# A gated mix of two attentions on one core: shift transfers one at a time, and the last four output rows spread over the last steps

## The chip, the cores and the metric

The kernel runs on one core of one Trainium2 chip. The metric is the device time of one execution in microseconds (us). Before the change it is 1537.48 us as the median of three runs (1534.87 to 1542.45). The engines of the core are TensorE (PE; its weight loads are PEld), VectorE (DVE), ScalarE (ACT), GpSimd (POOL) and SyncE (SP), which here only issues transfers.

## The reference

Both branches read the same `x` of 2048 rows by 512. Branch A is a sliding, dilated attention: each row attends to eight rows, itself and every second one behind it. Branch B is full attention of 32 query heads over one shared key and value head. A gate per row mixes the two outputs.

```python
S, D, H, Dh = 2048, 512, 32, 16
g = sigmoid((x * gate_w).sum(-1, keepdims=True))
# A: q, k, v per head from x @ wqkv; W = 8, dilation 2
logits = einsum("bhsd,bhswd->bhsw", q, k[pos - 2*w]) * Dh**-0.5   # masked where pos - 2*w < 0
a = (softmax(logits) weighted sum of v[pos - 2*w]) @ wo
# B: q per head from x @ wq, one k and v from x @ wk, x @ wv
b = (softmax(q @ k.T * Dh**-0.5) @ v) @ wo_b
return g * a + (1 - g) * b
```

Everything is float32. The queries and keys of B are large, so its softmax needs the row maximum taken off before the exponential.

## The kernel before

Float32 products of full accuracy are made from rounded parts: a high and a low half of each operand, and three products (high with high, high with low, low with high) added up in PSUM.

**Projections (to about 291 us).** A list of lumps, `lumps`, runs through the function `stream`: fourteen query lumps, then the lumps `("a", gg, j)`, where `gg` counts four groups of columns of branch A and `j` sixteen groups of 128 rows. A lump is twelve steps. In each step the two halves of the 128 contraction rows go as two matmuls on the two halves of the array (line 956) into the two halves of a PSUM pair, so the two halves must be added later. `a_post` does that after each lump: for the group `gg == 0` (which also carries the values of B and the gate's sums) ACT copies one half (line 241) and DVE adds the other half to it, three additions (lines 246, 248, 249). For the later groups `a_add` has ACT copy both halves (lines 265, 266) and POOL add them (line 272). The sum goes into a `stage` tile, of which there are two, each for two lumps, and every second lump the tile is stored to the DRAM buffer `ad`: from ACT's queue for group 0 (line 253), from SP's queue for the others (line 276). Branch A itself is computed later on POOL from `ad`.

**Maxima of branch B.** The scores of B are computed twice: once to find the maximum of each query row, once for the exponential. The first time is cut into 2048 *fills*; a fill is one 128 by 512 block of scores (line 330) and a reduction on DVE. They are not tied to a place: `stream` and the main loop put them wherever their planner finds a free PSUM bank. `fill_pair` does two at once in the bank `m2` (reduction line 350), `fill_one` a single one in the bank `m1` or another (line 361). During the projections of A another form is used, a *difference pass*: `fill_diff` forms half differences of two key blocks, ACT takes absolute values (line 418), and `fill_sum` adds half sums and reduces (line 428), so that one pass covers four fills. A unit `v` (there are 32, a quarter of the queries by four heads) has 64 fills. When they are done, `filled` sends its maxima through `shift_a` and `shift_c` (ACT, then POOL, which forms the tile `ml`) to `shift_b`, which writes them into rows 62 and 63 of the stacked queries `qst` by eight small transfers (line 449), issued at once. While branch A occupies POOL all eight go on SP's queue, later four on each. The exponentials of the unit may only start when its shift has been issued (`shifted`).

**Branch B.** The main loop has 512 steps and one more, sixteen for each unit. In a step `exp_pair` runs twice (scores on PE, line 460, exponential on ACT, line 462), and `weighted` adds the step before to the output (line 470, bank `po`). `fill_ready` adds up to one pair and one single fill a step. If the next unit's maxima would come too late, `pause` makes fills without exponentials. After each unit `finish_a`, `finish_b` and `finish_c` divide, gate and transpose its output; a unit is then `shaped`.

**Output rows.** `out_phase` multiplies four groups of 128 rows at a time with the output weights, as a block in which no exponential runs. For a row group, `prepare` splits branch B's part, `turn` transposes branch A's part, the products run through `stream` as two half matmuls each (line 731), with fills in between, and `out_store` has ACT copy both halves (line 666) and POOL add them. There are four blocks. In the last, the column block of the last two units is not yet there: its four sums are kept in `parts`, and the end of the kernel adds what is missing (line 1073) and stores.

**What sets the order.** The instruction order of each engine is written out by the planner when the program is built. It keeps planned clocks (`clk`, and `pool` for POOL), free times of banks (`free`) and a list `tasks` of due times, which `run_tasks` works off; it does not see the real times. Each engine and each queue then runs strictly in the written order.

## Time and profile before

| what | value |
|---|---|
| median of three runs | 1537.48 us |
| the profiled execution, its own time | 1539.43 us |
| span of its trace | 1537.6 us |
| mean granted clock of TensorE | 0.992 |
| PE, DVE, ACT, POOL busy | 1491.8, 1250.2, 1232.9, 1016.9 us |
| chain that ended last: PE, DVE, ACT, POOL | 85%, 5%, 4%, 2% |

The trace gives each instruction a start and a duration. Busy time is the time in which an engine executes; registers, semaphores and the issue of transfers are not counted. A matmul's record is longer than the distance to the next one, because matmuls overlap in the array: 0.40 us is listed for one that starts 0.24 us after its predecessor, so starts are to be compared. A wait names the instruction, what it waited for, the sum, the count and the longest, in us. Where the engine `SPq` or `POOLq` stands, it is the issue of a transfer. "Granted clock" is the share of its full rate at which TensorE was let run.

### The profile page before, as it was taken

What the parts mean: (1) busy time and instruction counts of PE and PEld (TensorE: products, weight loads), DVE (VectorE), ACT (ScalarE), POOL (GpSimd) and SP (SyncE); (2) the same over time, 40 slices, a digit from 0 to 9 for tenths busy, and PEclk for the clock granted to TensorE, in tenths of its full rate; (3) what the DMA queues carried; (4) which work ended last, traced back from release to release, by engine and by line L of the source; (5) the groups of instructions that cost most, each with busy time, mean ns of one, the idle gap of its engine ahead of it and who ended that gap; (6) DMA issues with size and microseconds to landing.
All of it is one profiled execution on the core that took longest, in us unless ns stands there. A gap on an engine that the chain in (4) does not pass through costs nothing.

```text
span 1537.6 us, 29033 instructions
## 1 busy us (share of the span) xinstructions
PE 1491.8 (97%) x11020; PEld 717.7 (47%) x11020; DVE 1250.2 (81%) x1794; ACT 1232.9 (80%) x1532; POOL 1016.9 (66%) x1725
## 2 busy tenths in 40 slices
PE   7999988999999999999999999999999999999997
PEld 4989878633333333333333453333453354333532
DVE  6987555688888889888898998888998899888821
ACT  4547766888999999999999759999759966998676
POOL 7833867888978888888988988888886132000320
PEclk9999989999999999999999999999999999999999
DMA  6743223220120211211211112202110000000000
GB/s 214 203 116 130 74 73 94 79 75 22 65 70 16 85 51 43 68 46 40 75 40 41 67 39 68 62 18 68 41 57 22 2 15 16 2 2 1 2 1 28
DMA packets 43908, 85.63 MB, mean 56 GB/s; under 512 B 9520, under 2 KB 25960, under 8 KB 39672
## 3 DMA queue, kind: packets, MB, share of 16 engines
q1 hardware_dynamic: 31976, 40.85, 8.9%
q0 software_dynamic: 6560, 37.95, 7.3%
q10 hardware_dynamic: 5232, 4.98, 1.0%
q8 instruction: 86, 1.41, 0.4%
q14 instruction: 54, 0.44, 0.1%
HBM read 57.97 MB, written 25.25 MB: 54 GB/s over the span
## 4 chain that ended last, share of the span: by engine, by line
PE 85%; DVE 5%; ACT 4%; POOL 2%; SPq 1%; DMA 1%; issue 1%; DVEq 0%; ACTq 0%; POOLq 0%
PE po L470 32%; PE pe L460 22%; PE pm L330 9%; PE ps L330 8%; PE pe L956 5%; PE pe L731 5%; ACT pexp L462 3%; DVE mx L350 3%; DVE mx L361 2%; SPq L449 1%; PE pe L174 1%; PE pm L409 1%; POOL stage L272 1%; DMA ad<-stage 1%; ACT dd L418 1%
## 5 line engine op out<-in xcount | busy, mean ns | idle before, releaser
L462 ACT ACTIVATE pexp<-pe 128x1024 f32<-128x1024 f32 x1024 | 991.7, 1022 | 98.8 <-PE pe L460 95.9
L350 DVE TENSOR_REDUCE mx<-pm 128x2 f32<-128x1024 f32 x563 | 687.1, 1220 | 125.1 <-PE pm L330 120.2
L470 PE MATMUL po<-pexp,vst 128*32 128x512 f32 x4096 | 545.5, 605 | 1.0 <-DVE tt L484 0.5
L460 PE MATMUL pe<-qst,kst 64*128 64x512 f32 x2048 | 464.8, 450 | 9.8 <-ACT pexp L462 4.8
L460 PEld LDWEIGHTS pe<-qst,kst 64*128 64x128 f32 x2048 | 191.3, 183 | 514.1 <-ACT pexp L462 500.5
L361 DVE TENSOR_REDUCE mx<-ps 128x1 f32<-128x512 f32 x568 | 385.8, 679 | 5.5 <-PE ps L330 4.7
L330 PE MATMUL pm<-kst,qst 62*128 62x512 f32 x1139 | 239.7, 408 | 2.3 <-DVE mx L350 1.8
L330 PE MATMUL ps<-kst,qst 62*128 62x512 f32 x568 | 230.6, 406 | 0.8 <-DVE mx L361 0.8
L530 POOL TENSOR_TENSOR pr<-aext 128x256 f32<-128x256 f32 x256 | 182.6, 741 | 2.6 <-DMA aext<-ad 2.4
L590 POOL TENSOR_TENSOR oa<-oa,av 128x256 f32<-128x256 f32 x224 | 164.3, 733 | 15.1
L470 PEld LDWEIGHTS po<-pexp,vst 128*32 128x32 f32 x4096 | 80.5, 108 | 179.4 <-issue 166.4
L587 POOL TENSOR_TENSOR av<-aext,lg 128x256 f32<-128x256 f32 x224 | 139.6, 623 | 13.5
L496 POOL TENSOR_TENSOR rl<-rl,gate_t 128x16 f32<-128x16 f32 x31 | 6.9, 222 | 180.5 <-DVE rl L490 180.3
L330 PEld LDWEIGHTS pm<-kst,qst 62*128 62x128 f32 x1139 | 110.4, 186 | 27.2 <-DVE mx L350 23.1
L330 PEld LDWEIGHTS ps<-kst,qst 62*128 62x128 f32 x568 | 105.7, 186 | 25.6 <-DVE mx L361 20.6
L956 PE MATMUL pe<-wah,xh 64*128 64x384 f32 (+1 forms) x504 | 112.0, 349 | 3.0 <-DVE gate L249 1.7
L956 PE MATMUL pe<-wah,xl 64*128 64x384 f32 (+1 forms) x504 | 112.7, 347 | 0.0
L428 DVE CUSTOM_DVE_ANT_0 dd<-ps,dd 128x512 f32<-128x512 f32 x78 | 53.9, 691 | 71.6 <-PE ps L409 36.9
L956 PE MATMUL pe<-wal,xh 64*128 64x384 f32 (+1 forms) x504 | 111.9, 345 | 0.0
L418 ACT ACTIVATE dd<-pm 128x512 f32<-128x512 f32 x156 | 85.3, 600 | 28.6 <-PE pm L409 26.5
L536 POOL TENSOR_TENSOR tr<-pr 128x512 f32<-128x512 f32 x64 | 81.7, 1277 | 4.3
L536 POOL TENSOR_TENSOR tr<-tr 128x256 f32<-128x256 f32 (+1 forms) x128 | 72.5, 567 | 8.6
(172 smaller groups left out, 1582.4 us busy)
## 6 DMA issues: line engine op xcount, KB each, us to landing
aext<-ad POOLq DMA_DIRECT2D x32, 1056.0 KB, 5.5
ad<-stage SPq DMA_DIRECT2D x24, 384.0 KB
qst<-qd SPq DMA_DIRECT2D x64, 128.0 KB
xraw<-xt SPq DMA_DIRECT2D x16, 256.0 KB
qd<-qhi SPq DMA_DIRECT2D x16, 256.0 KB
qd<-qlo SPq DMA_DIRECT2D x16, 256.0 KB
qst<-qd SPq DMA_DIRECT2D x64, 64.0 KB
qst<-ml SPq DMA_DIRECT2D x228, 2.0 KB
```

The source lines that it names most:

```text
L330: nc.tensor.matmul(dst, qst[v % NB][b:b + 62, pr, t * P:(t + 1) * P], kst[b:b + 62, kc * 512:(kc + 1) * 512], start=True, stop=True)
L350: nc.vector.tensor_reduce(m[:, :, pr, t, kc], dst, AX.X, ALU.max)
L361: nc.vector.tensor_reduce(m[:, odd, pr, t, kc:kc + 1], dst, AX.X, ALU.max)
L418: nc.scalar.activation(dd[0][:, odd], m2[:, odd, :], AF.Abs)
L460: nc.tensor.matmul(bank[:, odd, :], kst[b:b + 64, kt * P:(kt + 1) * P], qst[u % NB][b:b + 64, pr, :], start=True, stop=True)
L462: nc.scalar.activation(e, bank, AF.Exp, scale=SCALE)
L470: nc.tensor.matmul(po[32 * i:32 * i + 32, :], vst[:, kt, :], pexp[s, i // 2][:, i % 2, :], start=(kt == 0), stop=(kt == NJ - 1))
L530: nc.gpsimd.tensor_mul(pr[:, k], q, e[:, o:o + NH, AC:2 * AC])
L536: nc.gpsimd.tensor_add(nx, cur[:, :, 0:n], cur[:, :, n:2 * n])
L587: nc.gpsimd.tensor_mul(av, e[:, o:o + NH, 2 * AC:].rearrange("p j (h d) -> p j h d", d=DH), lg[:, w].unsqueeze(3).to_broadcast([P, NH, AG, ...
L590: nc.gpsimd.tensor_add(ao, ao, av)
L956: nc.tensor.matmul(front[2 if x == last else x % 2][0][:, b, :n], l[h], r[h], start=(i == 0), stop=(i == 3 * C - 1))
```

## The change

There are four edits.

1. `a_post` treats group 0 as it treats the others: ACT copies both halves to SBUF (and the narrow columns of the values and of the gate by two more copies), POOL adds them (three additions), and the store goes out on SP's queue. The planned durations become 1.2 us on ACT and 1.45 us on POOL. The old path through DVE, its tasks `post0` and `post1`, and the store on ACT's queue go away.
2. `shift_b` no longer issues its eight transfers at once. During the projections each becomes a task of its own, due 0.8 us after the one before (`shift_d`); in the main loop they are still issued together. The unit counts as shifted with the eighth.
3. In `stream`, a difference pass may be started when DVE's planned clock is up to 1.2 us ahead of PE's, in place of 0.7.
4. The last four row groups are no longer an `out_phase`. A generator, `spread`, gives out their products four at a time in each step of the main loop, as full 128-row matmuls into the two halves of `m2`, once all fills are done; `turn_all` transposes with four full transposes through `m1`, and ACT copies the finished row straight into `parts`. What is left after the last step runs then. The rule for single fills, now `singles`, is set to finish the fills at about step 488 of 512.

```diff
     def a_post(gg, j, x):
-        for kind in ("post0", "post1", "add") if not gg else ("post0", "post1"):
-            settle(kind, 0)
+        settle("add", 1)
...
         nc.scalar.activation(own, bank[:, 0, :GN].rearrange("p (g n) -> p g n", g=GC), AF.Copy)
-        nc.scalar.activation(two, bank[:, 1, :GN], AF.Copy)
-        at = after("act", clk["pe"] + T_LAT, 0.8)
+        nc.scalar.activation(two[:, :n], bank[:, 1, :n], AF.Copy)
+        if gg == 0:
+            nc.scalar.activation(vst[:, j, 0:DH], bank[:, 0, GN:GN + DH], AF.Copy)
+            nc.scalar.activation(gate[:, 1, j:j + 1], bank[:, 0, GN + DH:GN + DH + 1], AF.Copy)
+        at = after("act", clk["pe"] + T_LAT, 0.8 if gg else 1.2)
...
     def shift_b(v, ml):
-        for b in range(2):
-            dst = qst[v % NB][64 * b + 62:64 * b + 64].rearrange("x i (t q) -> x i t q", t=4).bitcast(F32)
-            for g in range(4):
-                (nc.gpsimd if b and not pieces else nc.sync).dma_start(...)
-        shifted.add(v)
+        for k in range(8):
+            if pe:
+                shift_d(v, ml, k)
+            else:
+                tasks.append((clk["pe"] + 0.8 * k, shift_d, (v, ml, k)))
...
-                if not half and not pend and max(free["m2"], clk["dve"] - 0.7) <= clk["pe"] + 0.1:
+                if not half and not pend and max(free["m2"], clk["dve"] - 1.2) <= clk["pe"] + 0.1:
                     fill_diff()
...
+    def spread(js, n):
+        m = 3 * (C + n)
+        def turn_all(j):
+            for c in range(C):
+                nc.tensor.transpose(m1[:, c * P:(c + 1) * P], oa[c // 2][:, j, c % 2 * P:(c % 2 + 1) * P], ident)
...
+        prepare(js[0], n)
+        yield 1.0
+        parts_a(js[0], *turn_all(js[0]))
+        yield 3.0
+        while slots or half:
+            yield 1.0
+        for j in js:
...
+                nc.tensor.matmul(m2[:, j % 2, :], st(), mv, start=(i == 0), stop=(i == m - 1))
...
+                if i == m - 6 and nxt:
+                    raw = turn_all(nxt)
+                yield 0.0
...
+            nc.scalar.activation(parts[j], m2[:, j % 2, :], AF.Copy)
...
+    def singles(s):
+        return 2 * max(0, 16 * (NU - 1) - 8 - s) + 11 * (NJ - 4 - outs) < to_go()
...
+        if outs == NJ - 4:
+            if NU - 3 in shaped and not half and not singles(s) and not later_rows and "last" not in done:
+                later_rows.append(spread(list(range(outs, NJ)), n))
+            if short > 0 and steps < 2:
+                pause(short)
...
-                ahead = 2 * (16 * (NU - 2) - 8 - s) + 11 * (NJ - 4 - outs)
-                if ahead < to_go() - NF // NU or s >= 16 * (NU - 2) - 8 and ahead + 64 < to_go():
+                if not later_rows and singles(s):
                     fill_ready("m1", M1S)
...
+        spread_some(4)
         if s:
             weighted(s - 1)
...
+    while later_rows:
+        clk["pe"] = max(clk["pe"], spread_at[0])
+        spread_some(99)
+        run_pool()
```

More of the change, by code (lines that the diff above doesn't have):

```diff
@@ L271, in rest @@
             nonlocal pool
-            nc.gpsimd.tensor_add(own, own, two.rearrange("p (g n) -> p g n", g=GC))
-            pool = max(pool, 1e3 * at) + 1000
+            nc.gpsimd.tensor_add(own, own, two[:, :GN].rearrange("p (g n) -> p g n", g=GC))
+            if gg == 0:
+                nc.gpsimd.tensor_add(vst[:, j, 0:DH], vst[:, j, 0:DH], two[:, GN:GN + DH])
+                nc.gpsimd.tensor_add(gate[:, 1, j:j + 1], gate[:, 1, j:j + 1], two[:, GN + DH:GN + DH + 1])
+            pool = max(pool, 1e3 * at) + (1000 if gg else 1450)
             if j % 2 == 1:
@@ L660, in gated_mix_kernel, with out_store @@
     parts, spare = {}, []
-    def out_store(j, n, k):
+    def out_store(j, k):
         nonlocal pool
@@ L668, in out_store @@
         pool = max(pool, 1e3 * clk["act"]) + 1300
[L669 to L680 removed]
+        nc.gpsimd.tensor_add(two[:, 0], two[:, 0], two[:, 1])
+        nc.sync.dma_start(out[0].rearrange("(p j) d -> p j d", j=NJ)[:, j, :], two[:, 0])
     def stream(seq, mm, done, pooled):
@@ L994, in gated_mix_kernel @@
     formed.clear()
-    for kind in ("post0", "post1", "add", "store"):
+    for kind in ("add", "store"):
         settle(kind, 0)
@@ L1047, in gated_mix_kernel @@
         run_pool()
-    assert not slots and not half and not hooks and not tasks and outs == NJ, (len(slots), len(hooks), len(tasks), outs)
+    while later_rows:
+        clk["pe"] = max(clk["pe"], spread_at[0])
+        spread_some(99)
+        run_pool()
+    assert not slots and not half and not hooks and not tasks and "last" in done, (len(slots), len(hooks), len(tasks), outs)
     for x in range(8):
```

93 lines of the change are left out of this document (53 added, 40 removed).

## The prediction

> **What bounds the kernel now.** I began with the page: share of busy time by engine, then the chain that ended last.
>
> ```profile
> PE 1491.8 (97%) x11020; PEld 717.7 (47%) x11020; DVE 1250.2 (81%) x1794; ACT 1232.9 (80%) x1532; POOL 1016.9 (66%) x1725
> ```
>
> TensorE (PE) is busy for 97% of the span, so a gain comes either from stretches where PE stands still, or from PE work that can lie under another engine. The change touches two places, so I went on with those: the projections of branch A (84 to 291 us) and everything behind the last sixteen-row unit (1412 us to the end).
>
> First place. The waits between 150 and 291 us have one entry that belongs to no engine:
>
> ```profile
> ACT stage L265 <- DMA ad<-stage: 18.5, 4, 7.0
> ```
>
> The same view of 158 to 172 us and of 282 to 300 us has the shortest two:
>
> ```profile
> ACT stage L265 <- DMA ad<-stage: 3.2, 1, 3.2
> ```
> ```profile
> ACT stage L265 <- DMA ad<-stage: 2.0, 1, 2.0
> ```
>
> Four times ScalarE (ACT) waits, 18.5 us in all, for a stage tile whose store to `ad` has not landed: 3.2, 7.0, 6.3 (what is left of the sum) and 2.0 us. The queue of SyncE (SP) says why (start, duration, what was issued; neighbours are merged):
>
> ```profile
> 158.16 5.23 SPq L449 DMA_DIRECT2D qst<-ml  x8
> 163.49 21.54 SPq L276 DMA_DIRECT2D ad<-stage  x5
> 195.70 5.22 SPq L449 DMA_DIRECT2D qst<-ml  x8
> 200.97 29.07 SPq L276 DMA_DIRECT2D ad<-stage  x6
> ...
> 276.18 5.56 SPq L449 DMA_DIRECT2D qst<-ml  x8
> 281.79 14.05 SPq L276 DMA_DIRECT2D ad<-stage  x4
> ```
>
> Four batches of eight small shift transfers (the one left out starts at 238.04) hold SP for 5.2 us each, 0.65 us per transfer, and a store is issued the moment the batch ends. ACT's own row answers it: issue at 200.97, work again at 203.77, so 2.8 us from issue to a free tile.
>
> ```profile
> 203.77 0.49 ACT L265 ACTIVATE stage<-pe 128x384 f32<-128x384 f32 x1 [7.01 <-DMA ad<-stage]
> ```
>
> What that does to PE is in busy time by stretch (busy us of PE, PEld, DVE, ACT, POOL, then the granted clock): the four batches, then a stretch without one.
>
> ```profile
> 157.00:177.00 20.00, 17.03 (x152) 16.04 (x150) 8.98 (x29) 13.46 (x31) 14.99 (x27) 0.83 0.24 71
> 195.00:215.00 20.00, 13.59 (x116) 12.91 (x116) 7.69 (x24) 9.17 (x21) 10.45 (x26) 0.74 0.27 81
> 237.00:257.00 20.00, 14.24 (x131) 13.60 (x129) 8.09 (x26) 10.21 (x22) 11.37 (x18) 0.83 0.36 115
> 276.00:291.00 15.00, 12.90 (x130) 11.75 (x128) 8.09 (x27) 11.16 (x24) 10.84 (x16) 1.00 0.26 81
> 215.00:235.00 20.00, 20.00 (x216) 19.40 (x214) 13.10 (x42) 17.92 (x41) 17.34 (x24) 1.00 0.23 70
> ```
>
> PE idles 3.0, 6.4, 5.8 and 2.1 us there, 17.3 us together, and not at all without a batch. After the three longer stops its clock is low as well:
>
> ```profile
> 168.70 0.52 PE L956 MATMUL pe<-wah,xl 64*128 64x384 f32 x2
> 169.02 0.52 PE L956 MATMUL pe<-wah,xh 64*128 64x384 f32 x2
> ...
> 174.50 0.34 PE L956 MATMUL pe<-wah,xl 64*128 64x384 f32 x2
> 174.67 0.34 PE L956 MATMUL pe<-wah,xh 64*128 64x384 f32 x2
> ```
>
> The pace is 0.32 us a pair at 168.70 and 0.17 at 174.50. Some 5.9 us from 168.1 on run at about half pace, a loss of 2.7 us; for three stops 8 us. After the fourth, whose wait was 2.0 us, the clock stayed at 1.00.
>
> Second place, the ordinary step of branch B while score maxima (fills) are still being placed, on PE:
>
> ```profile
> 1377.37 0.50 PE L460 MATMUL pe<-qst,kst 64*128 64x512 f32 x2
> 1377.70 0.40 PE L330 MATMUL pm<-kst,qst 62*128 62x512 f32 x2
> 1377.94 0.40 PE L460 MATMUL pe<-qst,kst 64*128 64x512 f32 x2
> 1378.18 0.40 PE L330 MATMUL ps<-kst,qst 62*128 62x512 f32 x1
> 1378.51 1.06 PE L470 MATMUL po<-pexp,vst 128*32 128x512 f32 x8
> 1379.50 0.50 PE L460 MATMUL pe<-qst,kst 64*128 64x512 f32 x2
> ```
>
> Start to start: 0.33 for scores, 0.24 for a pair of maxima, 0.24 for scores, 0.33 for a single one, 0.99 for the weighted sum, 2.13 us with no gap: PE-bound, three maxima a step. In the last steps the maxima are gone and ACT is the bound, two steps every 4.02 us:
>
> ```profile
> 1473.33 3.77 ACT L462 ACTIVATE pexp<-pe 128x1024 f32<-128x1024 f32 x4 [0.18 <-PE pe L460]
> 1477.35 3.77 ACT L462 ACTIVATE pexp<-pe 128x1024 f32<-128x1024 f32 x4 [0.25 <-PE pe L460]
> ```
>
> So 2.01 us a step, in which PE needs 0.33 + 0.24 + 0.99 = 1.56. Between the two regimes stands the block that the change dissolves: weighted sum 483, then number 484, with these reductions of maxima inside it.
>
> ```profile
> 1441.01 1.06 PE L470 MATMUL po<-pexp,vst 128*32 128x512 f32 x8
> ...
> 1471.79 1.07 PE L470 MATMUL po<-pexp,vst 128*32 128x512 f32 x8
> ```
> ```profile
> L350 DVE TENSOR_REDUCE mx<-pm 128x2 f32<-128x1024 f32 x13 | 15.9, 1226 | 0.4 <-PE pm L330 0.3
> L361 DVE TENSOR_REDUCE mx<-ps 128x1 f32<-128x512 f32 x14 | 9.5, 682 | 0.6 <-PE ps L330 0.6
> ```
>
> The block lasts 30.8 us, of which 2.0 would have been an ordinary step: 28.8 us. It also carries 2 x 13 + 14 = 40 maxima. Those have to go somewhere else.
>
> **The change part by part.** *Shift transfers one at a time.* In the projections the eight transfers become tasks 0.8 us apart, so a store that falls due gets its place after the first or second, not after the eighth. The count on SP stays 8. The first still waits on POOL for `ml`, and a store behind it waits too. Each store is then issued six to seven transfers earlier, 3.9 to 4.6 us. Of the four waits 3.2 and 2.0 vanish, the others shrink by about 4.6: 14.4 us. What remains (2.4 and 1.7) is near the 2.0 after which the clock stayed up, so I count all 8 us of low clock as saved. Term: -22.4. Bounds: all idle and all low clock gone, -25.3; a store that comes only one transfer earlier, -2.6.
>
> *Sums of the first A group from VectorE (DVE) to ACT and POOL; their stores from ACT's queue to SP's.*
>
> ```profile
> L241 ACT ACTIVATE two<-pe 128x402 f32<-128x402 f32 x16 | 8.1, 509 | 12.5 <-PE pe L956 6.3 <-DMA ad<-stage 3.6 <-DVE gate L249 2.1
> L246 DVE TENSOR_TENSOR stage<-pe,two 128x384 f32<-128x384 f32 x16 | 8.8, 549 | 0.8 <-ACT two L241 0.8
> L272 POOL TENSOR_TENSOR stage<-stage,two 128x384 f32<-128x384 f32 x48 | 48.7, 1016 | 22.1 <-ACT two L266 21.9
> ```
> ```profile
> 105.00:132.00 27.00, 26.68 (x269) 25.46 (x267) 21.64 (x78) 19.03 (x39) 3.78 (x6) 1.00 0.23 73
> ```
>
> DVE loses 0.55 us and two narrow adds per position, ACT gains a copy of 0.49 (the row at 203.77) and two narrow ones (0.9 us together, an estimate: no row has copies so narrow from PSUM), POOL gains an add of 1.02 and two narrow ones. POOL is busy 3.8 of 27 us there, so its work is hidden, and DVE was not the bound. ACT is at 19.0 of 27; about ten positions at 0.9 us bring it to 28, just over the stretch. I charge 2 us (0 if copies overlap, 9 if all of the 0.9 went on the path). The eight stores leave ACT's queue; on SP they meet only spread shifts.
>
> *The margin in the planner for difference passes (0.7 to 1.2), and the DVE time freed,* change how many maxima are placed before branch B. By the planner's own durations: 0.75 us freed in each of the first six positions at about 0.6 per maximum, +8; a pass that starts a step earlier, 5 passes of four in 48 positions, +20; ACT planned 1.2 instead of 0.45 in the first group, -10 to -15. I take +15 (0 to +35). Each pass costs PE about 0.3 us: +1.5 in all.
>
> *Four rows spread over the last steps.* The block goes: -28.8. The 84 products (21 for each row) become full 128-row matmuls, four a step. The nearest row, for the same shape:
>
> ```profile
> 1526.40 2.11 PE L1052 MATMUL pm<-woh 128*128 128x512 f32 x8
> ```
>
> Eight end to end take 2.11, the last one's length included: about 0.24 each. A step is then 0.33 + 0.24 + 4 x 0.24 + 0.99 plus two changes of tile shape at 0.09 (0.33 less 0.24 above), 2.70 us, PE-bound. For ACT, the copies of a row:
>
> ```profile
> L639 ACT ACTIVATE raw<-pe 128x512 f32<-128x512 f32 x16 | 9.6, 598 | 42.4 <-PE pe L633 39.2 <-POOL own L626 3.3
> ```
>
> Four of about this size in 21 / 4 steps are 0.46 a step, and the exponentials 3.77 / 2 = 1.89: 2.35, just beneath PE. So 21 steps x (2.70 - 2.01) = +14.5. [...] Were a change free, the term would be 21 x 0.51 = +10.7, and if ACT and PE did not overlap in half of the steps' copies, +19. Transposes and first preparation: +2. What is left after step 512: +1.4.
>
> *The 40 maxima of the block.* The new rule for singles (`2 x (488 - step) < to go`) lets twelve steps, 477 to 488, take one: +0.12 each, 1.5 us, and steps 485 to 488 take eight in pairs at no cost. Twenty are left at step 489, three fit, 17 go into a pause. A pause has been seen, five maxima long:
>
> ```profile
> 1412.86 1.06 PE L470 MATMUL po<-pexp,vst 128*32 128x512 f32 x8
> ...
> 1418.06 0.64 PE L470 MATMUL po<-pexp,vst 128*32 128x512 f32 x4
> ```
>
> 5.20 less 2.13 is 3.07 us, 0.61 per maximum. So 17 cost +10.4. The 15 gained above take off 9.2 (first the old pause of five, then ten of these).
>
> Sum: -22.4 + 2 + 1.5 - 28.8 + 14.5 + 2 + 1.4 + 1.5 + 10.4 - 9.2 = -27.1 us. The profiled execution took 1539.4 (span 1537.6 and 1.8 around it), so 1512.3; the median shown, 1537.48, is 1.9 lower, which would give 1510. I predict 1512.
>
> **The rivals.** *The tail gives nothing back.* No maxima are gained in front, 17 wait at step 489, and in that pause of some 10 us PE does a pair per 1.2 us. Then -9.2 and -1.5 fall away, and ACT's copies cost another 2: 1522. If so sparse a stretch drops the clock once, add the 2.7 of one stop above: 1524. [...] Chance 0.16.
>
> *The stores do not come earlier,* because the planner gives a store its place behind all eight, which its due time (up to 2.5 us ahead on POOL, plus 0.5) would allow if shifts go out in a bunch. For it: SP runs in written order. Against: tasks 0.8 us apart reach over 5.6 planned us, more than two lumps. Term -2.6 instead of -22.4: 1532. Chance 0.11.
>
> *Slower: the maxima run short.* Place: a pause at step 489 and the one at 473. Price 0.61 each. If ACT's longer duty in the first group lets the planner place fewer difference passes there (four maxima each), the pause grows. It decides from 27 / 0.61 = 44 missing, eleven passes: 1540 and above, say 1547 at 14. Against it: the margin of 1.2 works the other way in the 48 later positions. Chance 0.07.
>
> *Better:* all stops and both pauses gone: 1500 and less. Chance 0.04.
>
> **How the numbers follow.** The forecast has 0.62, reaching from 1500 to 1526 by the ends of its terms. Range 1500 to 1532: outside lie 0.04 below, 0.07 above for the shortage, and about half of the 0.11. A measurement of this kernel tells a change from none at about 0.5%, 7.7 us: faster means under 1530, slower over 1545. Faster: 0.62 + 0.16 + 0.03 of the second rival = 0.81, with 0.04 for better 0.85; I keep 0.82, since more than one term is unseen in any trace. Same: 0.11. Slower: 0.07.
>
> **What would show it.** Right: on SP no eight `ml` transfers in a row between 150 and 291 us; ACT's wait on `ad<-stage` under 5 us; granted clock 1.00 there; no block near the end, and 2.6 to 2.8 us a step in some 20 of the last 24 steps; reductions of maxima ended by about step 490. Wrong: the wait of 18.5 still there; PE gaps of over 10 us at step 489; steps of 3 us or more with products; the branch B loop starting later than before.

## The result, and the profile after

The changed kernel takes 1526.99 us as the median of six runs (1525.66 to 1528.23); the kernel before, in six runs beside it, 1537.49. The ratio is 0.9928, with a 95% interval of 0.9912 to 0.9945: faster by 10.5 us, which is more than the 0.5% that a measurement can tell, inside the range given, just beyond the 1526 us to which the forecast itself reached, and less than half of the 25.5 us forecast.

The profiled execution of the changed kernel took 1525.66 us, its span is 1523.8. One mark cuts the span in two: the transpose of the first unit's output (`tt<-po`). Up to it run the projections and the first unit; behind it run the other 31 units and the end of the kernel. Before, then after, from the timeline of DVE:

```profile
329.57 0.70 DVE L484 STREAM_TRANSPOSE tt<-po 128x512 f32<-128x512 f32 x1
```
```profile
314.37 0.71 DVE L472 STREAM_TRANSPOSE tt<-po 128x512 f32<-128x512 f32 x1
```

So the front gave 15.2 us, and the rest went from 1537.6 - 329.6 = 1208.0 to 1523.8 - 314.4 = 1209.4: the dissolved block brought nothing. My sum had -18.9 for the front (-22.4 + 2 + 1.5) and -8.2 for the rest. The two spans differ by 13.8 us and the medians by 10.5, because the profiled execution of the kernel before is 1.9 us above its median and that of the changed kernel 1.3 below.

**The front.** The waits between 150 and 291 us, one row of the kernel before, then two of the changed kernel:

```profile
PEld pm L409 <- ACT dd L418: 17.1, 6, 6.7
```
```profile
PEld pm L390 <- ACT dd L399: 11.6, 32, 1.6
...
ACT stage L240 <- DMA ad<-stage: 1.7, 2, 1.6
```

The 18.5 us of ACT's wait for the stage tile are 1.7. The row above it has changed its nature: PE's weight load for a difference pass waited 6 times for ACT to read the bank of the pass before, up to 6.7 us at a time, and now waits 32 times, 0.36 us each. The queue of SP shows a store inside a shift where eight transfers stood together:

```profile
191.76 3.91 SPq L436 DMA_DIRECT2D qst<-ml  x6
195.78 0.36 SPq L257 DMA_DIRECT2D ad<-stage  x1
196.19 1.26 SPq L436 DMA_DIRECT2D qst<-ml  x2
```

And the busy time by stretch (PE, PEld, DVE, ACT, POOL, then the granted clock) has no low clock any more, but PE now also idles 1.0 us from 215 to 235 us, where it was busy throughout before:

```profile
157.00:177.00 20.00, 19.78 (x200) 17.67 (x198) 13.22 (x42) 18.27 (x43) 17.96 (x33) 1.00 0.24 72
...
215.00:235.00 20.00, 18.97 (x192) 16.96 (x188) 12.77 (x42) 15.78 (x36) 16.24 (x26) 1.00 0.41 128
```

**The tail.** A step with products, on PE:

```profile
1453.63 1.06 PE L458 MATMUL po<-pexp,vst 128*32 128x512 f32 x8
1454.63 0.73 PE L448 MATMUL pe<-qst,kst 64*128 64x512 f32 x4
1455.29 0.73 PE L766 MATMUL pm<-wol,own 128*128 128x512 f32 x2
1455.86 0.63 PE L766 MATMUL pm<-woh,own 128*128 128x512 f32 x2
1456.42 1.06 PE L458 MATMUL po<-pexp,vst 128*32 128x512 f32 x8
```

2.79 us from start to start, without a gap: 1.00 for the weighted sum, 0.66 for four score products, 1.13 for four output products. The forecast was 2.70. Three times, where a row ends, the step is longer, by 2.2, 2.0 and 1.7 us. PE and ACT at the first of these places:

```profile
1466.81 1.94 ACT L450 ACTIVATE pexp<-pe 128x1024 f32<-128x1024 f32 x2 [0.84 <-PE pe L448]
...
1466.87 0.49 PE L766 MATMUL pm<-woh,turned 128*128 128x512 f32 x1
1468.63 0.60 ACT L781 ACTIVATE part<-pm 128x512 f32<-128x512 f32 x1
...
1469.29 0.97 PE L766 MATMUL pm<-woh,own 128*128 128x512 f32 x3 [1.92 <-ACT part L781]
```

The row's last product starts at 1466.87. The copy of the finished row (line 781) stands on ACT behind two exponentials and begins at 1468.63. The next row's first product goes into the other half of the bank pair `m2`, which nothing else uses then, but it starts only when the copy has ended. The waits of the end (1400 to 1525 us) have the sum:

```profile
PEld pm L766 <- ACT part L781: 6.2, 3, 2.2
PE pm L766 <- ACT part L781: 5.1, 3, 1.9
```

The second loss lies at the pause of fills ahead of the last unit, at step 488. PE, then the clock of the stretches around it:

```profile
1437.85 0.80 PE L448 MATMUL pe<-qst,kst 64*128 64x512 f32 x2 [1.77 <-DVE mx L331]
```
```profile
1434.00:1438.00 4.00, 1.91 (x13) 0.82 (x9) 3.72 (x5) 1.73 (x2) 0.00 (x0) 0.91 0.00 0
1438.00:1442.00 4.00, 4.00 (x16) 1.37 (x16) 0.69 (x1) 1.26 (x2) 0.00 (x0) 0.50 0.01 4
1442.00:1446.00 4.00, 4.00 (x25) 0.74 (x22) 1.19 (x3) 2.86 (x4) 0.00 (x0) 0.73 0.00 0
```

After a stop of 1.77 us PE ran at half rate for some 6.4 us (1437.85 to about 1444.2), a loss of 3.2 us.

### The profile page after: what moved, and what is told of

It reads as the page before. It is cut to its first block, busy times and chain, and to the rows that moved or that the text cites. A ratio compares the mean times of both kernels' runs of the same rounds, so it can differ in the third digit from the quotient of the medians.

```text
span 1523.8 us, 28901 instructions
## 1 busy us (share of the span) xinstructions
PE 1489.5 (98%) x10920; PEld 706.1 (46%) x10920; DVE 1235.3 (81%) x1755; ACT 1243.8 (82%) x1590; POOL 1030.6 (68%) x1769
## 4 chain that ended last, share of the span: by engine, by line
PE 89%; ACT 4%; DVE 4%; POOL 1%; issue 1%; DMA 1%; DVEq 0%; ACTq 0%; POOLq 0%
PE po L458 32%; PE pe L448 22%; PE pm L311 9%; PE ps L311 8%; PE pe L1004 8%; PE pe L709 4%; DVE mx L331 2%; ACT dd L399 2%; ACT pexp L450 1%; PE pm L766 1%; PE pm L390 1%; PE pe L174 1%; DVE mx L342 1%; PE po L390 0%; PE ps L390 0%
## 5 line engine op out<-in xcount | busy, mean ns | idle before, releaser
L331 DVE TENSOR_REDUCE mx<-pm 128x2 f32<-128x1024 f32 x554 | 676.6, 1221 | 125.7 <-PE pm L311 120.4
L311 PE MATMUL pm<-kst,qst 62*128 62x512 f32 x1122 | 235.7, 407 | 3.1 <-DVE mx L331 2.4
L311 PEld LDWEIGHTS ps<-kst,qst 62*128 62x128 f32 x565 | 105.3, 186 | 22.4 <-DVE mx L342 18.4
L399 ACT ACTIVATE dd<-pm 128x512 f32<-128x512 f32 x166 | 92.2, 610 | 21.8 <-DVE mx L409 10.8
L1004 PE MATMUL pe<-wah,xh 64*128 64x384 f32 (+1 forms) x504 | 108.5, 338 | 0.0
L1004 PE MATMUL pe<-wal,xh 64*128 64x384 f32 (+1 forms) x504 | 108.5, 337 | 0.0
L1004 PE MATMUL pe<-wah,xl 64*128 64x384 f32 (+1 forms) x504 | 108.4, 337 | 0.0
L409 DVE CUSTOM_DVE_ANT_0 dd<-ps,dd 128x512 f32<-128x512 f32 x83 | 57.4, 692 | 58.8 <-PE ps L390 29.4
L250 POOL TENSOR_TENSOR stage<-stage,two 128x384 f32<-128x384 f32 x64 | 65.0, 1015 | 26.3 <-ACT two L241 13.4
```

The costliest lines, as they stand in the source:

```text
L311: nc.tensor.matmul(dst, qst[v % NB][b:b + 62, pr, t * P:(t + 1) * P], kst[b:b + 62, kc * 512:(kc + 1) * 512], start=True, stop=True)
L331: nc.vector.tensor_reduce(m[:, :, pr, t, kc], dst, AX.X, ALU.max)
L399: nc.scalar.activation(dd[0][:, odd], m2[:, odd, :], AF.Abs)
L1004: nc.tensor.matmul(front[2 if x == last else x % 2][0][:, b, :n], l[h], r[h], start=(i == 0), stop=(i == 3 * C - 1))
```

## The experiments

Twelve more kernels were run. "First unit" is the mark above, "rest" the span less that mark; both come from the one profiled execution, and two executions of the same front differ by up to 2 us (314.4, 314.6 and 316.5 in the table; the last one, of e5, has the granted clock at 0.71 and 0.87 from 92 to 100 us, where the other two have 1.00). "Passes" is the number of difference passes in the program; each does the work of four fills. Ratios are to the kernel before, with their 95% intervals.

| kernel | passes | median us | ratio | first unit | rest |
|---|---|---|---|---|---|
| before | 78 | 1537.49 | 1 | 329.6 | 1208.0 |
| changed | 83 | 1526.99 | 0.9928 (0.9912 to 0.9945) | 314.4 | 1209.4 |
| e1 margin 0.7 | 73 | 1542.00 | 1.0033 (1.0018 to 1.0047) | 305.6 | 1234.2 |
| e2 shifts at once | 83 | 1528.40 | 0.9947 (0.9929 to 0.9965) | 317.9 | 1208.0 |
| e3 no row wait | 83 | 1522.04 | 0.9899 (0.9885 to 0.9914) | 314.6 | 1205.3 |
| e4 before, shifts only | 78 | 1519.03 | 0.9881 (0.9867 to 0.9896) | 307.8 | 1209.5 |
| e5 block at the end | 83 | 1522.06 | 0.9891 (0.9873 to 0.9910) | 316.5 | 1203.9 |
| e6 margin 1.3 | 84 | 1523.35 | 0.9896 (0.9878 to 0.9914) | 317.9 | 1204.0 |
| e7 old first group | 87 | 1526.08 | 0.9920 (0.9902 to 0.9937) | 324.6 | 1200.3 |
| e8 = e3 and e6 | 84 | 1517.24 | 0.9858 (0.9837 to 0.9879) | 319.2 | 1197.2 |
| e9 before, margin only | 87 | 1533.97 | 0.9968 (0.9958 to 0.9978) | 331.2 | 1200.0 |
| e10 before, first group only | 73 | 1541.09 | 1.0017 (1.0008 to 1.0026) | 315.7 | 1224.0 |
| e11 spread, passes held back | 84 | 1514.69 | 0.9846 (0.9826 to 0.9867) | 315.2 | 1197.1 |
| e12 = e11 with the block | 84 | 1518.26 | 0.9868 (0.9845 to 0.9891) | 316.8 | 1201.4 |

### What the transfers one at a time are worth

On the kernel before alone (e4):

```diff
     def shift_b(v, ml):
-        for b in range(2):
-            dst = qst[v % NB][64 * b + 62:64 * b + 64].rearrange("x i (t q) -> x i t q", t=4).bitcast(F32)
-            for g in range(4):
-                (nc.gpsimd if b and not pieces else nc.sync).dma_start(...)
-        shifted.add(v)
+        for k in range(8):
+            if pe:
+                shift_d(v, ml, k)
+            else:
+                tasks.append((clk["pe"] + 0.8 * k, shift_d, (v, ml, k)))
...
```

> The kernel before with one edit: the eight transfers of a shift are issued one at a time, 0.8 us apart. Passes and pauses stay the same in number. My term: 22.4 us below the kernel before (about 1515), the first unit's end at 307 us instead of 330 us, ACT's waits for the stage tile under 5 us, clock 1.00. Rival (the transfers are worth only what the changed kernel shows, 13 to 15 us): about 1523, the first unit's end at 315 us.

Measured: 1519.03 us, 18.5 below the kernel before; the first unit's end comes 21.8 us earlier, the span is 20.3 shorter. The wait, between 80 and 300 us:

```profile
ACT stage L265 <- DMA ad<-stage: 3.3, 3, 2.5
```

By the time it lies between my term and the rival; the first unit's end, which is where the edit works, is my 307 to within 1 us. The rest is 1.5 us longer although the program is the same there. At the old pause, with the same stop of PE, the clock stayed at 1.00 in the profile of the kernel before and fell in that of e4. PE and the clock, before:

```profile
1417.40 0.50 PE L460 MATMUL pe<-qst,kst 64*128 64x512 f32 x2 [1.77 <-DVE mx L350]
```
```profile
1416.00:1420.00 4.00, 2.60 (x21) 0.98 (x24) 2.44 (x4) 1.89 (x3) 0.00 (x0) 1.00 0.00 0
```

The same in e4:

```profile
1395.47 0.58 PE L467 MATMUL pe<-qst,kst 64*128 64x512 f32 x2 [1.77 <-DVE mx L350]
```
```profile
1396.00:1400.00 4.00, 4.00 (x21) 1.19 (x22) 1.57 (x3) 1.54 (x2) 0.00 (x0) 0.61 0.00 0
```

The same edit taken back from the changed kernel (e2):

```diff
     def shift_b(v, ml):
-        for k in range(8):
-            if pe:
-                shift_d(v, ml, k)
-            else:
-                tasks.append((clk["pe"] + 0.8 * k, shift_d, (v, ml, k)))
+        for b in range(2):
+            dst = qst[v % NB][64 * b + 62:64 * b + 64].rearrange("x i (t q) -> x i t q", t=4).bitcast(F32)
+            for g in range(4):
+                (nc.gpsimd if b and not pieces else nc.sync).dma_start(...)
+        shifted.add(v)
...
```

> The changed kernel with all eight transfers of a shift issued in one go again; everything else as changed, and the pauses and passes are the same in number. My term (22.4 us: 14.4 us of ACT's four waits for the stage tile and 8 us of lower clock): 20 to 25 us above the changed kernel, ACT's waits for the stage tile back at 15 us or more, and a clock beneath 0.95 between 133 us and 291 us. Rival (the transfers are worth only the 13 us by which groups 1 to 3 came out shorter): 11 to 15 us above it. A second rival (the stalls no longer fall where they did, since other things in the first phase have moved): under 8 us.

Measured: 1528.40 us, only 1.4 above the changed kernel (the intervals of the two overlap); the first unit's end is 3.5 later. In the waits between 80 and 300 us:

```profile
ACT stage L240 <- DMA ad<-stage: 6.4, 3, 2.8
```

So my term holds on the kernel before and not in the changed one: the transfers at once would hardly have stalled there. Two runs, each the kernel before with one edit, ask which of the others had taken the stall away. The margin alone (e9):

```diff
-                if not half and not pend and max(free["m2"], clk["dve"] - 0.7) <= clk["pe"] + 0.1:
+                if not half and not pend and max(free["m2"], clk["dve"] - 1.2) <= clk["pe"] + 0.1:
```

> The kernel before with one edit: the test of a difference pass at 1.2 instead of 0.7. Shifts go at once, the first A group is added by DVE, the last rows stay in a block; the program has 87 passes instead of 78 and no pause of 6 at step 472. The question is why transfers at once cost 22 us on the kernel before and 2 on the changed one. Theory 1 (the wider test spreads the passes otherwise, so the batches fall elsewhere between the stores): ACT's waits for the stage tile fall from 18.5 us to under 9 us, the first unit's end stands at 324 to 328 us, the time at 1527 to 1532. Theory 2 (it was the first A group's change that moved them): the waits stay at 14 us or more, the first unit's end comes at 335 us or later, and the time is 1538 or more.

Measured: 1533.97 us, the first unit's end at 331.2. The wait between 80 and 300 us:

```profile
ACT stage L265 <- DMA ad<-stage: 7.9, 3, 4.8
```

The first A group over ACT and POOL alone (e10):

```diff
     def a_post(gg, j, x):
-        for kind in ("post0", "post1", "add") if not gg else ("post0", "post1"):
-            settle(kind, 0)
+        settle("add", 1)
...
         nc.scalar.activation(own, bank[:, 0, :GN].rearrange("p (g n) -> p g n", g=GC), AF.Copy)
+        nc.scalar.activation(two[:, :n], bank[:, 1, :n], AF.Copy)
+        if gg == 0:
+            nc.scalar.activation(vst[:, j, 0:DH], bank[:, 0, GN:GN + DH], AF.Copy)
+            nc.scalar.activation(gate[:, 1, j:j + 1], bank[:, 0, GN + DH:GN + DH + 1], AF.Copy)
...
```

> The kernel before with one edit: the first A group goes over ACT and POOL as in the changed kernel. Shifts go at once, the test stays at 0.7, the rows in a block; the program has 73 passes instead of 78, and pauses of 11 and 22 fills at steps 456 and 472. Theory 1 of the run above: ACT's waits for the stage tile stay at 12 us or more, the first unit's end stands at 318 us or later (the run with the margin undone had 305.6 us with single transfers), the time at 1545 or more. Theory 2: the waits are under 8 us, the first unit's end stands by 311 us, the time at about 1536.

Measured: 1541.09 us, the first unit's end at 315.7. The wait in the same window:

```profile
ACT stage L240 <- DMA ad<-stage: 13.0, 4, 5.2
```

Neither theory has all of its numbers. By the wait, the margin alone takes 18.5 to 7.9, the first group's edit alone to 13.0, both together (e2) to 6.4: each takes a part, the margin the larger. The four pairs that differ in the transfers alone line up with it:

| others as in | wait at once | wait one at a time | first unit's end: gain of one at a time |
|---|---|---|---|
| before (before, e4) | 18.5 | 3.3 | 21.8 |
| first group's edit (e10, e1) | 13.0 | 5.4 | 10.1 |
| margin 1.2 (e9, e7) | 7.9 | 3.1 | 6.6 |
| both (e2, changed) | 6.4 | 1.7 | 3.5 |

In the first and third rows the gain is 1.4 times the wait saved, in the second 1.3, in the last 0.7, where the gain is not far from the 2 us by which executions differ. (e1 and e7 differ from e10 and e9 in the end of the kernel too, which lies behind the mark.) In all the forms at once a batch still holds SP for 5.2 us or a little more (5.22 to 5.57 in e2, e9 and e10). So what differs must be how the batches fall against the stores; why these edits shift them as they do was not tried.

### What the wider margin costs and brings

The changed kernel with the test at 0.7 again (e1):

```diff
-                if not half and not pend and max(free["m2"], clk["dve"] - 1.2) <= clk["pe"] + 0.1:
+                if not half and not pend and max(free["m2"], clk["dve"] - 0.7) <= clk["pe"] + 0.1:
```

> The changed kernel with the test before a difference pass put back from 1.2 to 0.7; everything else as changed. The program then has 73 passes in the first phase instead of 83, and the pauses of the last three units take 11, 22 and 18 fills instead of none, none and 6. Theory 1 (the wider test costs the first phase: in the changed kernel PE waits 12.5 us in 35 waits for ACT's absolute values, which the kernel before hardly does): the first unit's end comes 7 to 14 us earlier than in the changed kernel, and the 45 fills that are back in pauses cost 45 x 0.61 = 27 us, so the time is 13 to 20 us above the changed kernel (about 1540 to 1547). Theory 2 (the wider test costs nothing, as its 0.3 us for each of ten passes in my sum says): the first unit's end comes at most 3 us earlier, and the time is 24 us or more above the changed kernel.

Measured: 1542.00 us, 15.0 above the changed kernel. The first unit's end is 8.75 us earlier with ten passes fewer, so a pass costs 0.87 us and not the 0.3 of my sum. It is rather more: e1's profiled execution has the clock low in the front (0.78 and 0.79 from 92 to 100 us, 0.60 from 172 to 176), where the changed kernel has 1.00. By these windows that is about 3 us, an estimate, and without it a pass comes to 1.2. The rest is 24.8 us longer, which is 40 fills at 0.62, or 0.55 for the 45 that are back in pauses; either holds low clock behind e1's long pauses as well (0.52 from 1408 to 1412 us, 0.55 from 1456 to 1460). Theory 1 holds. Where the price of a pass goes, in the waits between 80 and 300 us:

```profile
PEld pm L390 <- ACT dd L399: 3.8, 6, 2.1
```

With the wide test it was 13.6 us in 39 waits in the same window. The planner lets a pass out when its own clocks say that ACT has read the bank; ACT is later than that, and PE, which works in written order, stands. A run with a term against that, built on the best form so far: the first group as in the kernel before, the margin at 1.3, the rows of the next section, and a pass held back 0.15 behind the planned reading (e11, against e8 further below; its other edits left out):

```diff
-                if not half and not pend and max(free["m2"], clk["dve"] - 1.3) <= clk["pe"] + 0.1:
+                if not half and not pend and max(free["m2"] + 0.15, clk["dve"] - 1.3) <= clk["pe"] + 0.1:
```

> Single transfers and the spread rows with DVE's copy and the later start of the next row, with the first A group as in the kernel before, the test at 1.3 and a new term in it: a difference pass goes out only 0.15 after the planner's time at which ACT has read the bank. The program has 84 passes and no pause at step 488, as the kernel with 1.3 and no row wait (1517.2). Theory (with the wide test PE waits 0.36 us a pass for ACT's absolute values, because the pass goes out too early): the waits of PE's weight loads on ACT's absolute values fall from 13 us to under 9 us, the first unit's end comes 3 to 6 us earlier than the 319 us there, and the time is 1512 to 1515. Rival (the passes cost what they cost, wherever they stand): first unit's end within 2 us, time within 2 us of 1517.

Measured: 1514.69 us, with the same 84 passes as e8.

```profile
PEld pm L409 <- ACT dd L418: 6.8, 19, 0.8
```

The wait fell from 14.5 us (e8, same window) to 6.8, the first unit's end from 319.2 to 315.2, the rest stayed (1197.2 and 1197.1). The wait does what the theory says. That the time does is not shown. The run changed the first group's path as well, and e8's profiled execution has the clock low twice in the front (0.82 and 0.75 from 92 to 100 us, 0.74 and 0.83 from 236 to 244), which e11's has not; by these windows that is about 3 of the 4.0 us, an estimate. Two of e8's four executions had a mean clock of 1.00, and they took 1515.58 and 1516.30 us.

A better price of a pass comes from e12 (further below), whose program differs from e4's in this test alone: six passes more, and the first unit's end 9.0 us later; in e11, with the same front as e12, it is 7.4. So a pass that is held back still costs 1.2 to 1.5 us, and one that is not 1.9 (e7 against e4, nine passes, 16.8 us). Where a pass stands is a part of its price. From e4 to e11, whose front is e12's, PE's weight loads wait only 2.7 us more for the absolute values (4.1 to 6.8), and what else makes a pass dear the runs leave open.

The first group's path taken back from the changed kernel alone (e7):

```diff
     def a_post(gg, j, x):
...
+        if gg:
+            return a_add(gg, j, x, st, bank, key)
...
+        tasks.append((at, rest, (), f"post{x % 2}"))
```

> The changed kernel with the first A group's results added by DVE again, as before; all else as changed. The program has 87 passes instead of 83 and no pause at step 488. What the pause costs by the margin's run (3 to 5 us) is gained in any case, and four passes cost 4 x 0.87 = 3.5 us. My term (ACT and POOL cost 2 us more than DVE): the first unit's end comes within 2 us of the changed kernel's 314.4 us. Rival (the first group is quicker by ACT and POOL, by the 1.8 us that its stretch was shorter): the first unit's end comes 4 to 6 us later.

Measured: 1526.08 us, within the spread of the changed kernel; the first unit's end 10.2 us later, with four passes more, and the rest 9.1 us shorter. Both numbers missed: four passes at 0.87 explain 3.5 of the 10.2. In the same window the wait on ACT's absolute values is 17.9 us in 46 waits instead of 13.6 in 39. What the first group's path costs by itself stays open, since each setting of it brings its own number of passes.

### What the spread rows are worth

The changed kernel with the last rows in the block (e5):

```diff
-        if outs == NJ - 4:
-            if NU - 3 in shaped and not half and not singles(s) and not later_rows and "last" not in done:
-                later_rows.append(spread(list(range(outs, NJ)), n))
...
+        if due or outs < NJ and outs // NH in done and (NHG * (k + 1) - 1 in shaped if n == C else s >= 16 * (NU - 2) + 4) and (lead < LEAD or s >= 16 * (NHG * (k + 2) + 1) - 3):
...
-        spread_some(4)
```

> The changed kernel with the last four rows in one block again (at step 484, with 40 of the last unit's fills inside it) and no products given out in the steps; shifts, first A group, margin and the 83 passes as changed. My terms for this part (block 28.8 saved; 14.5 for 21 longer steps, 2 for the transposes, 1.4 behind the last step and 1.5 for singles paid, and a pause of 6 fills for 3.7): the spread is worth 5 to 6 us net, so this kernel comes out 5 to 6 us above the changed one. Theory now (row waits of 2.2 us three times and a low clock worth 3 us behind the pause eat that up): this kernel is 0 to 4 us below the changed one, about 1523 to 1527, and the time from the end of the unit at s=464 to the end is under 141 us.

Measured: 1522.06 us, 4.9 below the changed kernel. The spread, as it was made, is a loss, and the sign of my term was wrong. Is it the row waits? Two edits together: the copy of a finished row goes to DVE, and the next row's products start a step later (e3):

```diff
-            nc.scalar.activation(parts[j], m2[:, j % 2, :], AF.Copy)
-            after("act", clk["pe"] + T_LAT, 0.5)
+            nc.vector.tensor_copy(parts[j], m2[:, j % 2, :])
+            after("dve", clk["pe"] + T_LAT, 0.5)
             if nxt:
                 parts_a(nxt, *raw)
+            yield 0.5
```

> The changed kernel with two edits in the spread rows: the finished row is copied out of the bank by DVE instead of by ACT behind two exponentials, and the next row's first products go out one step later. Theory (the three waits of 2.2 us at the row ends are ACT's queue and nothing else): the waits on the copy go, two to six products more are left behind step 512 at 0.25 us each, and the time falls by 4.5 to 6 us (about 1521 to 1522.5). Rival (something else is late just behind it, ACT's copy of the turned row or POOL's subtraction): the waits change their name, and the time falls by less than 2 us.

Measured: 1522.04 us, 5.0 below the changed kernel, as expected, though seventeen products instead of eight are left behind the last weighted sum, nine more where two to six were expected. At the first row end:

```profile
1466.90 0.49 PE L766 MATMUL pm<-woh,turned 128*128 128x512 f32 x1
...
1467.33 1.06 PE L458 MATMUL po<-pexp,vst 128*32 128x512 f32 x8
1467.43 0.69 DVE L781 COPY part<-pm 128x512 f32<-128x512 f32 x1 [6.06 <-PE pm L766]
1468.32 1.00 PE L448 MATMUL pe<-qst,kst 64*128 64x512 f32 x4
...
1469.25 0.97 PE L766 MATMUL pm<-woh,own 128*128 128x512 f32 x3
```

DVE copies during the weighted sum, and the next row starts without a wait. Which of the two edits does how much was not tried. Between 1460 and 1480 us PE is busy for 19.99 of 20 us, where the changed kernel had 18.08.

Then the pause. At 1.3 the same program has one pass more, and no fills are left for a pause (e6):

```diff
-                if not half and not pend and max(free["m2"], clk["dve"] - 1.2) <= clk["pe"] + 0.1:
+                if not half and not pend and max(free["m2"], clk["dve"] - 1.3) <= clk["pe"] + 0.1:
```

> The changed kernel with the test of a difference pass at 1.3 in place of 1.2. The program then has 84 passes instead of 83, and the pause of 6 fills at step 488 is gone; the spread rows and all else stay. Theory (the pause costs its idle 1.8 us, and the clock at half for 6.5 us behind it another 3.2 us): no window below a clock of 0.98 between 1420 and 1460 us, the time 4 to 5 us below the changed kernel less 0.9 us for the pass, so 3 to 4 us (about 1523). Rival (the low clock belongs to the serial preparation of the first row and comes anyway): the clock falls again in that stretch and the time is within 1.5 us of the changed kernel.

Measured: 1523.35 us, 3.6 below the changed kernel; first unit 3.6 later, rest 5.4 shorter. (The span is only 1.9 shorter: this profile has the clock at 0.84 and 0.73 from 92 to 100 us, which the changed kernel's has not.) The preparation of the first row, which the rival blamed, now runs at full clock, but the clock fell elsewhere, behind two of the three row waits. PE, then the clock around the first:

```profile
1462.76 1.04 PE L766 MATMUL pm<-woh,own 128*128 128x512 f32 x3 [1.92 <-ACT part L781]
```
```profile
1460.00:1464.00 4.00, 2.08 (x12) 0.87 (x12) 0.00 (x0) 2.92 (x4) 0.73 (x1) 0.94 0.00 0
1464.00:1468.00 4.00, 4.00 (x20) 1.32 (x16) 0.00 (x0) 1.51 (x2) 0.54 (x1) 0.64 0.00 0
1468.00:1472.00 4.00, 4.00 (x26) 1.50 (x28) 0.00 (x0) 2.61 (x4) 0.00 (x0) 1.00 0.01 2
```

Both edits together (e8):

```diff
-                if not half and not pend and max(free["m2"], clk["dve"] - 1.2) <= clk["pe"] + 0.1:
+                if not half and not pend and max(free["m2"], clk["dve"] - 1.3) <= clk["pe"] + 0.1:
...
-            nc.scalar.activation(parts[j], m2[:, j % 2, :], AF.Copy)
+            nc.vector.tensor_copy(parts[j], m2[:, j % 2, :])
...
+            yield 0.5
```

> The changed kernel with the margin at 1.3 and with the rows' copy on DVE and the next row's products one step later. If both causes are separate, the gains add: 4.9 us and 3 to 4 us, so about 1518 to 1519. If the row waits only moved the end of the same slack, less than 6 us in all.

Measured: 1517.24 us, 9.75 below the changed kernel; 5.0 and 3.6 make 8.6, so the gains add, to within the scatter of e8 (1515.58 to 1518.80). With neither row waits nor the pause the clock stays at 1.00 from 1420 to 1500 us.

Last, the block again on the front of e11 (e12), so that the cured spread stands against the block:

```diff
-        spread_some(4)
...
+    def out_store(j, n, k):
...
+            parts[j] = spare[x]
+            nc.gpsimd.tensor_add(parts[j], two[:, 0], two[:, 1])
```

> The kernel of the run before this one (1514.7 us) with the last four rows in a block again: single transfers, first A group by DVE, test at 1.3 with the 0.15 after ACT's reading, 84 passes, 40 fills inside the block, no pause. The first phase is the same program. Theory (without row waits and without a pause in front of it, the spread is worth what my terms for it said, 5 to 7 us): 1519.5 to 1522. Rival (the spread is worth nothing even so, and the gain of that run came from its first phase alone): within 2 us of 1514.7.

Measured: 1518.26 us against 1514.69, so the cured spread is worth 3.6 us (4.3 by the rests), less than the 5 to 7 expected, and more than nothing. Against e4, which differs in the test for the passes alone, e12 gains 0.8 us, and the executions of the two overlap (1517.91 to 1520.05 and 1518.44 to 1520.27): the wider test, even with passes held back, pays for itself and no more. So of the 22.8 us that e11 is below the kernel before, 18.5 are the single transfers and 3.6 the cured spread. Busy time between 1460 and 1480 us of e11, then of e12:

```profile
1460.00:1480.00 20.00, 19.99 (x116) 8.38 (x116) 0.69 (x1) 15.31 (x18) 3.47 (x3) 1.00 0.00 1
```
```profile
1460.00:1480.00 20.00, 18.71 (x122) 5.17 (x122) 0.97 (x2) 18.79 (x21) 0.84 (x2) 1.00 0.00 1
```

There the bound is seen to change hands: in the spread PE is full and ACT has air; behind the block ACT is busy for 18.79 of 20 us, and PE waits for it.

## Why the prediction was right and wrong

The sign of the whole was right, and the time lies in the range. The size was 2.4 times too large, 25.5 us forecast against 10.5, and the rest of the kernel, forecast at -8.2, got 1.4 longer: there the sign was wrong.

By steps from kernel to kernel the median of 1537.5 goes down 18.5 with the transfers alone (e4), up 3.0 with the first group and the margin (e5), and up 4.9 with the spread rows (changed). The single transfers alone are 8.0 us better than the whole change. My sum had -22.4; then +3.5 in front and about -3 for the old pause of fills that goes; then -28.8 + 14.5 + 2 + 1.4 + 1.5 = -9.4 for the spread, with pauses on top.

*Shifts, -22.4.* Right on the kernel before (-21.8 at the first unit's end, -20.3 in the span). "I count all 8 us of low clock as saved" held: every stretch of the projections is at 1.00, in e4 and in the changed kernel. The step that failed is adding this to the other edits as if they left that stall alone. They had taken two thirds of it themselves (18.5 to 6.4 us of wait), at a price of their own.

*Margin: "Each pass costs PE about 0.3 us: +1.5 in all."* Measured 0.87 for each of ten, about 1.2 without e1's low clock, and 1.2 to 1.5 from e4 to e11 and e12. The 0.3 had no row behind it, and no run shows it. It was to price the pass's own work and named nobody who waits for it; the bank's reader, ACT, was late, and PE's queue stood 39 times. That is a part of the price; the rest of it is open. In exchange the fills came out much as forecast: five passes more, twenty fills, against the +15 of the sum, and 0.62 us each where they spare a pause, against 0.61, though that this agrees so well is luck, since the 0.62 holds low clock and the 0.61 does not.

*Both together in the front:* -15.2 measured against -18.9, so the two errors largely cancelled there; that the front came out near its sum is luck. Of the +2 for the first group, the 0.9 us of ACT per position, an estimate, is what the rows of the changed kernel give (means of 0.495, 0.202 and 0.203 us for the copy of 384 and the two narrow ones); what it costs the path no run shows by itself.

*Spread rows.* The block is as long as the sum had it (30.83 us in e12, from 1421.46 to 1452.29). The step that failed is "2.35, just beneath PE": I added up ACT's load per step and did not ask what stands behind what in its queue. A copy that PE needs at once stood behind two exponentials (1.94 us), and the next row's first product waited for it: 2.2, 2.0 and 1.7 us, 5.9 together. Taking that away gave 5.0 us (4.1 by the rest), though nine of the products put off by a step come to run behind the last weighted sum, which at some 0.25 each (four take 1.04 us in the changed kernel, 1511.28 to 1512.32) costs 2.2 us. With it away the spread is worth 4.3 us by the rests (e11 against e12) where the sum had 9.4; these 2.2 and the 1.9 of the longer steps below leave about 1 us open. I had also not listed who waits for `m2`: the two halves were counted as two banks, and the written program waits for the pair as one.

*The pause.* "A pause has been seen" was used as a price of 0.61 per fill, and no low clock was added. The pause of the changed kernel had the same six fills as the old one (five and the step's own), and this time the clock fell: 3.2 us more. The length of the pause does not bring that by itself: behind the old pause, after a stop of PE of 1.77 us both times, the clock fell in e4 and not in the profile of the kernel before, and in e2, with the same pause as in the changed kernel, it was at 0.65 and 0.50 from 1442 to 1446 us and back at 0.99 then, which costs about 1.7 us. The rival "the tail gives nothing back" had one such drop in it, and its 1524 came nearest of the four; but its mechanism, 17 fills in a sparse pause of 10 us, did not occur.

*Product steps, 2.70.* Measured 2.79: the four score products take 0.66 (1454.63 to 1455.29) and not 0.33 + 0.24, which was read from steps where maxima stand between the two pairs. The 0.09 that the sum charged to a change of tile shape (0.33 less 0.24) was my estimate, and no run shows it by itself. In this step 0.33 stands four times, at both pairs of scores and at the first and the last output product, where the sum had it three times. Over 21 steps the difference is 1.9 us. The end behind the last weighted sum had +1.4: its start to the end of the span was 1537.6 - 1525.4 = 12.2 us and is 1523.8 - 1510.3 = 13.5 now, +1.3.

The rest of the kernel adds up: -8.2 forecast, +5.9 row waits, +3.2 clock, +1.9 longer steps, and -1.2 because the pause is as long as the old one and not two fills longer (10.4 - 9.2): +1.6, against +1.4 measured.

Of the signs named beforehand, the wait under 5 us, the clock at 1.00, the vanished block and the end of the reductions near step 490 came true. The length of the steps did so in part: of the 18 from 1453.6 to 1510.3 us eleven take 2.77 to 2.79 us, where some 20 were expected. Six take more than 3 us, which was a sign of being wrong: three with transposes in them (3.23), and the three row ends (4.97, 4.75, 4.51). Between 150 and 291 us one batch of eight still stood together on SP, at 289.27, behind the last store.

## What to carry to other kernels

An engine's load per step does not say when it delivers: for every result that another engine needs at once, list what stands in front of it in its engine's written order, and who stands behind the waiter. A stall that depends on where a batch falls between two stores is worth what it costs only on the kernel where it was measured; before adding its cure to other edits that move the same queue, ask what they leave of it. When work is moved out of a block, give its copies to the engine that the block had kept busy and that now stands idle (here DVE, busy for 18.25 of 20 us from 1420 to 1440 in e12, with the block, and for 0.69 of 20 from 1460 to 1480 in e11, with the spread; 0.69 us a copy, tried together with a later start of the next row).

## What was not expected of the hardware

Stops of PE of nearly the same length were answered differently by the clock. After 1.77 us (the pause of the changed kernel) it ran at 0.50 for about 6.4 us; after 1.92 us at a row end of e6 at 0.64 over the next 4 us, and after 1.46 us at the last row end there at 0.70 between 1496 and 1500 us; after the row waits of 1.92, 1.69 and 1.46 us in the changed kernel it stayed at 1.00. The drop behind the pause came again in e3, with the weighted sums at 1.93 instead of 1.06 us. Nor does the program decide it: the same pause was followed by 1.00 in the profile of the kernel before and by 0.61 over 4 us in e4, and the same front ran at 1.00 from 92 to 100 us in the changed kernel and in e3, and at 0.71 and 0.87 in e5. So a sum can give such a drop a chance and a size, here up to 3.2 us, but cannot read it off the length of one stop; what does decide, the runs leave open.
